# State times w_in formed once per batch, outputs accumulated tile by tile in a written order, weights converted on three engines

## The chip, the cores and the metric

The kernel runs on one core of one Trainium2 chip. The core has five engines that run side by side, each with its own strict queue: TensorE (PE; its weight loads are listed as PEld), VectorE (DVE), ScalarE (ACT), GpSimd (POOL) and SyncE (SP, which issues the transfers here). The metric is the device time of one execution in microseconds (us), lower is better. Before: 1142.45 us, the median of 3 runs (1141.72 to 1147.12).

## The reference

Two blocks. The first is a cross attention between 512 tokens and 32 state rows, for 8 batches and 8 heads of width 64, both ways round; the second is a feed-forward block with the gate h cos h over all 8 x (512 + 32) rows.

```python
# x (8, 8, 512, 64), state (8, 8, 32, 64): batch, head, row, width
scores = scale * np.matmul(x, state.transpose(0, 1, 3, 2))
a = softmax(scores)                       # over the 32 state rows
xread = np.matmul(a, state)
scores2 = scale * np.matmul(state, x.transpose(0, 1, 3, 2))
a2 = softmax(scores2)                     # over the 512 tokens
sread = np.matmul(a2, x)
attn = np.concatenate([xread, sread], axis=2)
# heads side by side: (8 * 544, 512)
x = attn.transpose(0, 2, 1, 3).reshape(B * S, H * D)
h = x @ w_in                              # w_in (512, 2048)
g = h * np.cos(h)
out = g @ w_out                           # w_out (2048, 512)
```

Everything is fp32 but w_in and w_out, which come as fp64 and are turned into fp32 on the chip.

## The kernel before, in words

**Attention** of a batch (`attention`, L120 to L233) transposes the states (L126) and the tokens (L134), forms the scores both ways (L150: state by token, L165: token by state), subtracts maxima, takes one Exp over both (L177), normalizes, and transposes the weights back (L197 into `a2T`, L205 into `aT`). L215 then reads tokens with the state's weights into `sT`, which collects what the states of all batches read. L228 multiplies the token's weights with the state: this gives `xx`, 512 features by 512 tokens, in four tiles of 128 features.

**Feed-forward** of a batch (`ffn`, L256). The hidden layer has 2048 features, in 16 tiles `f` of 128. For a tile, `gated` (L235) does four matmuls (L238), one for each 128 of the 512 contracted features, into a PSUM bank `hp`. The gate follows: DVE forms `q` (L242, L244) and `r` (L246, L248), ACT takes Abs and Sin (L250, L251), and DVE multiplies with `hp` into `g` (L253). All 16 `g` of a batch are kept (`gp` has 18 buffers). Then, for each 128 tokens, 16 matmuls (L265) add up one output tile in a PSUM bank; two banks are used in turn. ACT copies it out (L269) and SP stores it. After the eight batches the same is done for the 256 rows of `sT`, the state batch.

**Weights** (`load_w`, L89). A tile of 128 x 512 fp64 numbers is loaded as pairs of 32-bit words (`raw`, three buffers). Six DVE operations, one on ACT and one on POOL rebuild the number in fp32: `e` (L102, L104, L105, L107) carries sign and exponent, `fr` (L111, L112, L113) one plus the fraction, and POOL multiplies them (L115). There are 32 such tiles: 16 of `w_in` and 16 of `w_out`.

**Order.** The program writes attention of batch 0, the conversion of `w_in`, and then, for each batch, attention of the next batch before the feed-forward of this one; the conversion of one tile of `w_out` is written behind each hidden tile of batch 0. The framework's scheduler then sets the order on each engine. The PSUM banks are split 3 (`aps`, attention) + 3 (`hps`, hidden) + 2 (`ops`, outputs). SP's queue is written in the order: the first half of x of batch 0, states, the rest of it, weights, x of batch 1 between them; the loads of x (`load_x`, L78) for batch b + 2 are asked for at the start of batch b.

Of the kernel before, what the change touches and what calls it, by code (L numbers as in the profile page):

```python
# [9 lines left out]
F32 = mybir.dt.float32  # L10
# [16 lines left out]
def kernel(  # L27
# [18 lines left out]
    T = S + Ns            # tokens of a batch in the output  # L46
# [3 lines left out]
    wraw = ctx.enter_context(tc.tile_pool(name="wraw", bufs=3))  # L50
    xin = ctx.enter_context(tc.tile_pool(name="xin", bufs=3))
    asb = ctx.enter_context(tc.tile_pool(name="asb", bufs=1))
    small = ctx.enter_context(tc.tile_pool(name="small", bufs=2))
    xxp = ctx.enter_context(tc.tile_pool(name="xxp", bufs=2))
    gp = ctx.enter_context(tc.tile_pool(name="gp", bufs=NF + 2))
    msb = ctx.enter_context(tc.tile_pool(name="msb", bufs=2))
# [6 lines left out]
    halfpi = consts.tile([P, 1], F32)  # L63
    nc.vector.memset(halfpi, math.pi / 2.0)
# [3 lines left out]
    stB = consts.tile([P, B, NHB, 2 * D], F32)  # L68
    nc.vector.memset(stB, 0.0)
    st_src = state.rearrange("b (hb q) n d -> q n b hb d", q=4)  # L70
    for q in range(4):
        j = q % 2
        nc.sync.dma_start(out=stB[Ns * q:Ns * q + Ns, :, :, D * j:D * j + D],
                          in_=st_src[q])

# [11 lines left out]
    WC = 512  # L87

    def load_w(dst, src):  # L89
        """fp32 dst [P, WC] from src: fp32, or fp64 as its bits in 64-bit words."""  # L90
        if src.dtype == F32:
            nc.sync.dma_start(out=dst, in_=src)
            return
        raw = wraw.tile([P, WC, 2], I32, name="raw")
        nc.sync.dma_start(out=raw.rearrange("p f w -> p (f w)"),
                          in_=src.bitcast(I32))
        hi = raw[:, :, 1]
        lo = raw.bitcast(U32)[:, :, 0]
        # A power of two with the number's sign and exponent (zero below the
        # fp32 range, infinite above it), times 1 + its fraction.  # L100
        e = msb.tile([P, WC], I32, name="e", tag="q", bufs=3)
        nc.vector.tensor_scalar(e, hi, 20, 0x7FF, op0=ALU.logical_shift_right,  # L102
                                op1=ALU.bitwise_and)
        nc.vector.tensor_scalar(e, e, 896.0, 1151.0, op0=ALU.max, op1=ALU.min)  # L104
        nc.vector.tensor_scalar(e, e, 896.0, 2.0 ** 23, op0=ALU.subtract,  # L105
                                op1=ALU.mult)
        nc.vector.scalar_tensor_tensor(out=e, in0=hi, scalar=-2 ** 31, in1=e,  # L107
# [8 lines left out]

    # What attention writes to the state, of all batches: (j d) x pair x token.
    sT = consts.tile([P, NK, B, Ns], F32)

    def attention(b):  # L120
        x_b = x_t.pop(b)

# [208 lines left out]
```

## Time and profile before

| | |
|---|---|
| Time, median of 3 runs | 1142.45 us (1141.72 to 1147.12) |
| Profiled execution, first to last instruction | 1139.7 us |
| PE hidden matmuls, 128 x 512 (L238) | 1024 instructions, busy 448.8 us |
| PE output matmuls (L265) | 1088 instructions, busy 471.9 us |
| PE matmuls of L228 | 64 instructions, busy 23.4 us |
| DVE operations of conversion, L111 (the costliest) | 32, busy 26.2 us |
| POOL product, L115 | 32, busy 24.9 + 22.6 us |
| Bytes moved | 35.13 MB, mean 31 GB/s |

The profiled execution is one run of the program, and its span is the time from its first to its last instruction; the device time of a run also holds what lies around it. A busy time is the union of a group's instructions, a mean is the duration of one: PE's instructions overlap, so a mean of 592 ns does not say how far apart two of them start. An fp32 matmul stands as two instructions in the profile. In the list of groups, "xN" is the number of instructions, and what follows the second bar is the idle time of the engine before them with what ended it.

### The profile page before, as it was taken

How to read it: one execution, taken by the hardware profiler on the slowest of the kernel's cores; microseconds unless marked ns; L12 is line 12 of the kernel's file. 1: busy time of each engine (PE TensorE's matmuls, PEld its weight loads, DVE VectorE, ACT ScalarE, POOL GpSimd, SP SyncE). 2: the span in 40 equal slices, each digit the busy share in tenths (PEclk: the TensorE clock that was granted, in tenths of full speed). 3: DMA queues.
4: the chain of work that ended last, by engine and by line, in shares of the span. 5: the costliest groups of instructions: out<-in, count | busy, mean ns of one | idle time of the engine just before them, and what ended most of it. 6: DMA issues, size and time to landing. Idle time of an engine off the chain costs nothing.

```text
span 1139.7 us, 8231 instructions
## 1 busy us (share of the span) xinstructions
PE 1073.4 (94%) x3152; PEld 527.0 (46%) x3152; DVE 627.8 (55%) x1090; ACT 290.1 (25%) x440; POOL 48.2 (4%) x38
## 2 busy tenths in 40 slices
PE   3816999999999999999999999999999999999998
PEld 2504334554446444554455444544455444444483
DVE  6999998088107950488008830587028820791080
ACT  2313224043103320233013320243023310341041
POOL 1331222000000000000000000000000000000000
PEclk8967999999999999999999999999999999999999
DMA  9543221020001000010000000000000000000000
GB/s 203 156 138 93 92 93 38 18 37 1 9 19 39 8 8 20 10 37 1 18 19 1 0 10 18 10 1 1 18 19 1 0 10 18 10 0 17 20 1 19
DMA packets 45031, 35.13 MB, mean 31 GB/s; under 512 B 36544, under 2 KB 36544, under 8 KB 44992
## 3 DMA queue, kind: packets, MB, share of 16 engines
q1 hardware_dynamic: 44992, 34.61, 10.9%
q8 instruction: 25, 0.41, 0.2%
q14 instruction: 14, 0.11, 0.0%
HBM read 25.69 MB, written 8.91 MB: 30 GB/s over the span
## 4 chain that ended last, share of the span: by engine, by line
PE 84%; DVE 13%; issue 1%; DMA 1%; SPq 0%; ACT 0%; POOL 0%; ACTq 0%
PE o L265 39%; PE h L238 36%; PE at L215 2%; PE at L165 2%; DVE e L107 2%; PE at L228 2%; DVE e L104 1%; DVE fr L113 1%; DVE e L102 1%; PE at L150 1%; DVE e L105 1%; PE at L197 1%; DVE r L246 1%; PE at L134 1%; PE at L205 1%
## 5 line engine op out<-in xcount | busy, mean ns | idle before, releaser
L265 PE MATMUL o<-w_out,g 128*128 128x512 f32 x1088 | 471.9, 592 | 1.6 <-POOL w_out L115 1.6
L238 PE MATMUL h<-xx,w_in 128*128 128x512 f32 x1024 | 448.8, 595 | 4.8 <-DVE g L253 4.5
L265 PEld LDWEIGHTS o<-w_out,g 128*128 128x128 f32 x1088 | 206.4, 190 | 260.9 <-issue 255.9
L238 PEld LDWEIGHTS h<-xx,w_in 128*128 128x128 f32 x1024 | 191.8, 190 | 246.6 <-issue 214.3
L242 DVE TENSOR_SCALAR q<-h 128x512 f32<-128x512 f32 (+1 forms) x144 | 94.9, 659 | 131.3 <-PE h L238 128.8
L250 ACT ACTIVATE r<-r 128x512 f32<-128x512 f32 (+1 forms) x144 | 87.4, 607 | 297.2 <-DVE r L248 294.0
L128 DVE COPY stT<-at 128x256 f32<-128x256 f32 x8 | 3.4, 426 | 253.1 <-PE at L126 253.1
L269 ACT COPY ot<-o 128x512 f32<-128x512 f32 x34 | 19.9, 585 | 386.6 <-PE o L265 386.6
L253 DVE TENSOR_TENSOR g<-h,r 128x512 f32<-128x512 f32 (+1 forms) x144 | 94.9, 659 | 33.5 <-ACT r L251 31.1
L251 ACT ACTIVATE r<-r,halfpi 128x512 f32<-128x512 f32 (+1 forms) x144 | 100.6, 699 | 4.3
L248 DVE SCALAR_TENSOR_TENSOR r<-q,r 128x512 f32<-128x512 f32 (+1 forms) x144 | 95.0, 660 | 4.0
L246 DVE SCALAR_TENSOR_TENSOR r<-q,h 128x512 f32<-128x512 f32 (+1 forms) x144 | 93.5, 650 | 1.1
L244 DVE TENSOR_SCALAR q<-q 128x512 f32<-128x512 f32 (+1 forms) x144 | 58.7, 408 | 3.7
L197 PE MATMUL at<-ident,z 128*128 128x128 f32 x64 | 10.1, 310 | 42.6 <-DVE z L184 42.6
L165 PEld LDWEIGHTS at<-stT,xT 128*128 128x128 f32 x256 | 29.3, 192 | 8.5 <-PE at L150 5.7
L112 ACT ACTIVATE fr<-fr 128x512 f32<-128x512 int32 x32 | 19.9, 623 | 48.9 <-DVE fr L111 48.9
L156 DVE TENSOR_REDUCE mx<-at 128x1 f32<-128x512 f32 x16 | 11.0, 686 | 38.3 <-PE at L150 38.3
L232 ACT COPY xx<-at 128x512 f32<-128x512 f32 x32 | 17.6, 588 | 56.3 <-PE at L228 56.3
L165 PE MATMUL at<-stT,xT 128*128 128x64 f32 x256 | 30.6, 277 | 1.1 <-DVE z L157 1.1
L197 PEld LDWEIGHTS at<-ident,z 128*128 128x128 f32 x64 | 8.7, 161 | 46.7 <-issue 46.7
L215 PEld LDWEIGHTS at<-a2T,x_b 128*128 128x128 f32 x256 | 29.6, 193 | 0.5 <-DVE aT L207 0.3
L215 PE MATMUL at<-a2T,x_b 128*128 128x64 f32 x256 | 29.6, 274 | 0.0
(45 smaller groups left out, 482.0 us busy)
## 6 DMA issues: line engine op xcount, KB each, us to landing
x_b<-in_x_dram SPq DMA_DIRECT2D x32, 256.0 KB, 4.6
raw<-in_moe_w_in_dram SPq DMA_DIRECT2D x16, 512.0 KB, 4.1
raw<-in_moe_w_out_dram SPq DMA_DIRECT2D x16, 512.0 KB, 3.3
out_dram<-ot SPq DMA_DIRECT2D x32, 256.0 KB, 2.0
stB<-in_state_dram SPq DMA_DIRECT2D x4, 128.0 KB, 3.9
out_dram<-ot SPq DMA_DIRECT2D x8, 64.0 KB, 1.7
```

What stands on the lines that cost most here:

```text
L165: nc.tensor.matmul(out=s1[:, ci * H + 2 * k:ci * H + 2 * k + 2, :], lhsT=xT[:, k, CH * ch + ci, :], rhs=stT[:, k // 2, 64 * e:64 * e + 64] ...
L197: nc.tensor.transpose(out=tp[:, c, :], in_=z2[:, hb, P * c:P * c + P], identity=ident)
L215: nc.tensor.matmul(out=sr[:, k, :], lhsT=x_b[:, c, 2 * k:2 * k + 2, :], rhs=a2T[:, k // 2, c, 64 * e:64 * e + 64], start=(c == 0), stop=(c ...
L238: nc.tensor.matmul(out=hp, lhsT=w_in[:, k, P * f:P * f + P], rhs=xx[:, k, :], start=(k == 0), stop=(k == NK - 1))
L242: nc.vector.tensor_scalar(q, hp, 1.0 / (2.0 * math.pi), MAGIC, op0=ALU.mult, op1=ALU.add)
L244: nc.vector.tensor_scalar(q, q, MAGIC, None, op0=ALU.subtract)
L246: nc.vector.scalar_tensor_tensor(out=r, in0=q, scalar=-C1, in1=hp, op0=ALU.mult, op1=ALU.add)
L248: nc.vector.scalar_tensor_tensor(out=r, in0=q, scalar=-C2, in1=r, op0=ALU.mult, op1=ALU.add)
L250: nc.scalar.activation(r, r, func=ACTF.Abs)
L251: nc.scalar.activation(r, r, func=ACTF.Sin, bias=halfpi, scale=-1.0)
L253: nc.vector.tensor_tensor(g[:, 0:n], hp, r, op=ALU.mult)
L265: nc.tensor.matmul(out=op, lhsT=g[f][:, P * t:P * t + P], rhs=w_out[:, f, :], start=(f == 0), stop=(f == NF - 1))
```

## The change

- **Hidden layer.** Instead of forming `xx` = state x weights first and contracting it with `w_in` over 512 features, the state is multiplied with `w_in` once per batch (`products`, new L290): `sw`, 256 rows (head, state row) by 2048. The hidden matmuls (`hidden`, new L319) then contract the token's weights `aT` with `sw` over 256 rows, two matmuls a tile instead of four. L228 and its four copies on ACT are gone; eight product parts a batch and their eight copies on ACT (new L298) are new. The state batch still contracts `sT` with `w_in` over 512.
- **Outputs.** Four PSUM banks hold the four output tiles of a batch; as soon as a hidden tile has its `g`, four matmuls add its share to all four (`output`, new L352). `gp` has 4 buffers instead of 18. The banks are split 2 + 2 + 4.
- **Written order.** The scheduler is switched off, and the program's order is each engine's order. Attention is cut into 19 parts and the products into 8; for each hidden tile about 1.7 of these parts for the next batch are written between the steps: `gate3` of the tile before (its product with the Sin), `hidden`, `gate` (q), parts, `gate2` (r, Abs, Sin), `output` of the tile two back, parts.
- **Conversion.** ACT does three steps (a Relu for the exponent's lower bound, and the two halves of the fraction), POOL adds the halves and multiplies, DVE does four steps instead of six. The first half of a conversion is written with the second half of the one before. Four tiles of `w_in` are converted within attention of batch 0, and two tiles with each hidden tile of batch 0, `w_in` and `w_out` by turns. In batch 0 the subtraction of `q` is on ACT. `raw` has four buffers, `e`, `fr` and `fl` two each.
- **Loads.** The state loads stand first on SP, then x of batch 0, four weight tiles, x of batch 1; each further weight tile is fetched behind a conversion's second half. `x_b` has two buffers instead of three.

The core of the diff:

```diff
-    aps = ctx.enter_context(tc.tile_pool(name="aps", bufs=3, space=PSUM))
-    hps = ctx.enter_context(tc.tile_pool(name="hps", bufs=3, space=PSUM))
-    ops = ctx.enter_context(tc.tile_pool(name="ops", bufs=2, space=PSUM))
+    aps = ctx.enter_context(tc.tile_pool(name="aps", bufs=2, space=PSUM))
+    hps = ctx.enter_context(tc.tile_pool(name="hps", bufs=2, space=PSUM))
+    ops = ctx.enter_context(tc.tile_pool(name="ops", bufs=4, space=PSUM))
+    ctx.enter_context(tc.manual_schedule())
...
+            e = cvt.tile([P, WC], I32, name="e")
+            nc.vector.tensor_scalar(e, hi, 20, 0x7FF,
+                                    op0=ALU.logical_shift_right,
+                                    op1=ALU.bitwise_and)
+            nc.scalar.activation(e, e, func=ACTF.Relu, bias=ebias)
+            fr = cvt.tile([P, WC], F32, name="fr")
+            fi = fr.bitcast(I32)
+            nc.vector.tensor_scalar(fi, hi, 0xFFFFF, None, op0=ALU.bitwise_and)
+            nc.scalar.activation(fr, fi, func=ACTF.Copy, scale=2.0 ** -20,
+                                 bias=1.0)
+            fl = cvt.tile([P, WC], F32, name="fl")
+            nc.scalar.activation(fl, lo, func=ACTF.Copy, scale=2.0 ** -52)
+            half[i] = (hi, e, fr, fl)
+        if i - 1 in half:
+            hi, e, fr, fl = half.pop(i - 1)
+            nc.gpsimd.tensor_tensor(fr, fr, fl, op=ALU.add)
+            nc.vector.tensor_scalar(e, e, 255.0, 2.0 ** 23, op0=ALU.min,
+                                    op1=ALU.mult)
+            nc.vector.scalar_tensor_tensor(out=e, in0=hi, scalar=-2 ** 31,
+                                           in1=e, op0=ALU.bitwise_and,
+                                           op1=ALU.bitwise_or)
+            nc.gpsimd.tensor_tensor(loads[i - 1][0], fr, e.bitcast(F32),
+                                    op=ALU.mult)
+            fetch(i - 1 + 5)
...
+        def products(nt, hb):
+            ps = aps.tile([P, WC], F32, name="at")
+            for e in range(2):
                 nc.tensor.matmul(
+                    out=ps[64 * e:64 * e + 64, :],
+                    lhsT=stT[:, hb, 64 * e:64 * e + 64],
+                    rhs=w_in[:, 2 * hb + e, WC * nt:WC * nt + WC],
+                    start=True, stop=True, tile_position=(0, 64 * e))
+            nc.scalar.copy(sw[:, hb, WC * nt:WC * nt + WC], ps)
...
+    def output(t):
+        nt = t.n // P
+        if t.f == 0:
+            for i in range(nt):
+                acc[i] = ops.tile([P, Dm], F32, name="o")
+        for i in range(nt):
+            nc.tensor.matmul(out=acc[i], lhsT=t.g[:, P * i:P * i + P],
+                             rhs=w_out[:, t.f, :],
+                             start=(t.f == 0), stop=(t.f == NF - 1))
...
+        for t in tiles(b):
+            if line:
+                gate3(line[-1])
+            hidden(t)
+            gate(t)
+            line.append(t)
+            want = (len(work) * (t.f + 1) + NF - 1) // NF
+            mid = (n_done + want + 1) // 2
+            while n_done < mid:
+                work[n_done]()
+                n_done += 1
+            if b == 0:
+                convert_to(NK + 1 + 2 * (t.f + 1))
+                if t.f % 4 == 3:
+                    for part in first[:NHB]:
+                        part()
+                    first = first[NHB:]
+            gate2(t)
+            if len(line) > 2:
+                output(line.pop(0))
+            while n_done < want:
+                work[n_done]()
+                n_done += 1
```

Two places in the engines' orders. The first is TensorE's queue. Before, a whole batch from one L126 to the next (batch 2 and the attention of batch 3) stands as long runs; "at" are attention's PSUM tiles, "o" the outputs, and x50 is a run of 50 matmuls:

```order
L126 MATMUL at<-ident,stB 128x128 x2
L134 MATMUL at<-ident,x_b 128x128 x16
L150 MATMUL at<-xT,stT 64x512 x4
L165 MATMUL at<-stT,xT 128x64 x16
L238 MATMUL h<-xx,w_in 128x512 x13
L197 MATMUL at<-ident,z 128x128 x8
L238 MATMUL h<-xx,w_in 128x512
L205 MATMUL at<-ident,z 128x128 x8
L215 MATMUL at<-a2T,x_b 128x64 x16
L228 MATMUL at<-aT,stB 128x512 x4
L238 MATMUL h<-xx,w_in 128x512 x50
L265 MATMUL o<-w_out,g 128x512 x64
```

After, in the same queue, tiles 10 and 11 of a later batch with attention's last parts and the first products for the next (L278 is the old L215, L293 a product part, L322 the hidden and L358 the output matmuls):

```order
L322 MATMUL h<-aT,sw 128x512 x2
L278 MATMUL at<-a2T,x_b 128x64 x8
L358 MATMUL o<-w_out,g 128x512 x4
L278 MATMUL at<-a2T,x_b 128x64 x8
L322 MATMUL h<-aT,sw 128x512 x2
L293 MATMUL at<-w_in,stT 64x512 x2
L358 MATMUL o<-w_out,g 128x512 x4
L293 MATMUL at<-w_in,stT 64x512 x2
```

The runs of 64 hidden and 64 output matmuls have become groups of 2 and 4, with one part of the next batch's work behind each; L228 is gone, and L293 stands in its place.

The second place is VectorE's queue in batch 0, while weights are converted. Before, with the numbers of the buffers and the semaphores that each row waits for, one hidden tile and one conversion:

```order
L105 TENSOR_SCALAR e_779<-e_779 128x512 [waits DVE_49]
L111 TENSOR_SCALAR fr_784<-raw_777 128x512
L107 SCALAR_TENSOR_TENSOR e_779<-raw_777,e_779 128x512 [waits DVE_49]
L242 TENSOR_SCALAR q_794<-h_789 128x512 [waits PE_49,Pool_49]
L253 TENSOR_TENSOR g_775<-h_762,r_770 128x512 [waits Activation_49]
L113 SCALAR_TENSOR_TENSOR fr_784<-raw_777,fr_784 128x512 [waits Activation_49]
L244 TENSOR_SCALAR q_794<-q_794 128x512 [waits DVE_49]
L102 TENSOR_SCALAR e_806<-raw_804 128x512 [waits DMAHW0_49]
L246 SCALAR_TENSOR_TENSOR r_797<-q_794,h_789 128x512 [waits DVE_49]
L104 TENSOR_SCALAR e_806<-e_806 128x512 [waits DVE_49]
L248 SCALAR_TENSOR_TENSOR r_797<-q_794,r_797 128x512 [waits DVE_49]
```

After, one hidden tile (the eighth) with its two conversions, from its q on:

```order
L328 TENSOR_SCALAR q_725<-h_722 128x512 [waits PE_49]
L258 COPY a2T_333<-at_728 128x512 [waits PE_49]
L138 TENSOR_SCALAR e_734<-raw_658 128x512 [waits DMAHW3_49,Pool_49]
L144 TENSOR_SCALAR fr_737<-raw_658 128x512
L153 TENSOR_SCALAR e_697<-e_697 128x512
L155 SCALAR_TENSOR_TENSOR e_697<-raw_644,e_697 128x512 [waits DVE_49]
L138 TENSOR_SCALAR e_748<-raw_695 128x512 [waits DMAHW4_49,Pool_49]
L144 TENSOR_SCALAR fr_751<-raw_695 128x512
L153 TENSOR_SCALAR e_734<-e_734 128x512 [waits Activation_49]
L155 SCALAR_TENSOR_TENSOR e_734<-raw_658,e_734 128x512 [waits DVE_49]
L338 SCALAR_TENSOR_TENSOR r_770<-q_725,h_722 128x512
L340 SCALAR_TENSOR_TENSOR r_770<-q_725,r_770 128x512 [waits DVE_49]
```

Before, steps of the gate and of one conversion alternate, and a conversion's `e` waits only for its load; now the eight steps of two conversions stand between q and r, and each first step (L138) waits for POOL as well.

More of the change, by code (lines that the diff above doesn't have):

```diff
@@ new lines, in convert @@
+    def convert(i):
+        if not f64:
+            return
+        if i < len(loads):
+            raw = raws.pop(i)
+            hi = raw[:, :, 1]
+            lo = raw.bitcast(U32)[:, :, 0]
+            e = cvt.tile([P, WC], I32, name="e")
[22 more added lines that the diff above has]
+            fetch(i - 1 + 5)
@@ new lines, in reads @@
+        def reads(half):
+            if half == 0:
+                sr[0] = aps.tile([P, NK, 2 * Ns], F32, name="at")
+            for k in range(2 * half, 2 * half + 2):
+                e = k % 2
+                for c in range(NC):
+                    nc.tensor.matmul(
+                        out=sr[0][:, k, :], lhsT=x_b[:, c, 2 * k:2 * k + 2, :],
+                        rhs=a2T[:, k // 2, c, 64 * e:64 * e + 64],
+                        start=(c == 0), stop=(c == NC - 1))
+            if half == 0:
+                return
+            for j in range(2):
+                rows = slice(D * j, D * j + D)
+                nc.vector.tensor_copy(sT[rows, :, b, :],
+                                      sr[0][rows, :, Ns * j:Ns * j + Ns])
@@ L251, in gated @@
         nc.scalar.activation(r, r, func=ACTF.Sin, bias=halfpi, scale=-1.0)
[L252 to L270 removed]
+        t.r = r
@@ L304 @@
+    gate3(line[-1])
+    for t in line:
+        output(t)
 _INS = ['x', 'state', 'moe_w_in', 'moe_w_out']
```

301 lines of the change are left out of this document (168 added, 133 removed).

## The prediction

> **What bounds the kernel now.** I read the page's first two parts, then the chain that ended last, then busy time by stages that I cut by hand at the joints of the program, then TensorE's instructions in order of time.
>
> ```profile
> span 1139.7 us, 8231 instructions
> PE 1073.4 (94%) x3152; PEld 527.0 (46%) x3152; DVE 627.8 (55%) x1090; ACT 290.1 (25%) x440; POOL 48.2 (4%) x38
> PE   3816999999999999999999999999999999999998
> PEclk8967999999999999999999999999999999999999
> PE 84%; DVE 13%; issue 1%; DMA 1%; SPq 0%; ACT 0%; POOL 0%; ACTq 0%
> ...
> 0.00:36.70 36.70, 17.60 (x110) 14.96 (x110) 25.21 (x44) 7.55 (x10) 4.81 (x9) 0.86 0.82 184
> 36.70:195.00 158.30, 115.87 (x348) 54.28 (x346) 155.47 (x281) 49.56 (x79) 43.43 (x29) 0.89 0.33 100
> 195.00:340.51 145.51, 145.51 (x399) 68.41 (x399) 58.54 (x96) 31.37 (x45) 0.00 (x0) 1.00 0.07 20
> 466.34:592.17 125.83, 125.83 (x372) 60.90 (x371) 62.19 (x102) 32.21 (x47) 0.00 (x0) 1.00 0.07 17
> ```
>
> The last four rows are stretches with busy time of PE, PEld, DVE, ACT and POOL, the clock, and DMA. Two regimes show. Up to 195 us the weights are converted: DVE is busy 155.5 of 158.3 us, and nearly all of PE's 66 idle us lie before that point. From 195 us PE is busy in every microsecond at full clock, and DVE and ACT are half idle and a quarter busy. So behind 195 us time is worth what PE's instructions are worth; before it, what DVE's queue is worth.
>
> ```profile
> 466.34 0.38 PE L126 MATMUL at<-ident,stB 128*128 128x128 f32 x2
> 468.42 1.95 PE L150 MATMUL at<-xT,stT 128*64 128x512 f32 x8
> 491.36 2.92 PE L228 MATMUL at<-aT,stB 64*128 64x512 f32 x8
> 494.21 43.18 PE L238 MATMUL h<-xx,w_in 128*128 128x512 f32 x100
> 592.17 0.38 PE L126 MATMUL at<-ident,stB 128*128 128x128 f32 x2
> ...
> 969.64 55.10 PE L238 MATMUL h<-xx,w_in 128*128 128x512 f32 x128
> 1024.58 55.10 PE L265 MATMUL o<-w_out,g 128*128 128x512 f32 x128
> 1093.49 5.34 PE L238 MATMUL h<-sT,w_in 128*128 128x256 f32 x24
> 1098.67 1.02 PE L265 MATMUL o<-w_out,g 128*128 128x512 f32 x2
> ```
>
> An fp32 matmul is two instructions here: a batch has 16 x 4 hidden matmuls and 128 rows of L238. 128 of them take 1024.58 - 969.64 = 54.94 us, 0.429 us each; L265 costs the same. From one L126 to the next a batch takes 125.83 us. The state batch's 256-wide ones cost (1098.67 - 1093.49) / 24 = 0.216 us.
>
> **A batch on PE after.** The hidden layer contracts over 256 instead of 512: 64 instructions fewer, -64 x 0.429 = -27.5 us. L228 goes: -2.9 us. Added are 8 product parts, each two matmuls of 64 columns, that is four instructions. Their nearest row is L150, the same shape and the same column positions: 8 instructions in 1.95 us, so 0.98 us for four. That is about half of 4 x 0.429 = 1.72 us, so the two column halves run beside each other. Bounds 0.86 to 1.72 us a part; I take 1.0, since the shape is the same: +8 us. The parts of attention now stand singly between hidden and output matmuls. L150's 0.98 against 0.86 says that a change of shape costs about a tenth of a microsecond; ten such changes a batch beyond those of before are 1 us (0 to 4.5). Sum: 125.8 - 27.5 - 2.9 + 8 + 1 = 104.5 us, an estimate, 6.5 us a tile.
>
> This holds if the others keep up within a tile.
>
> ```profile
> L251 ACT ACTIVATE r<-r,halfpi 128x512 f32<-128x512 f32 x128 | 92.5, 723 | 3.8
> L248 DVE SCALAR_TENSOR_TENSOR r<-q,r 128x512 f32<-128x512 f32 x128 | 88.3, 690 | 3.8
> L253 DVE TENSOR_TENSOR g<-h,r 128x512 f32<-128x512 f32 x128 | 88.3, 689 | 32.5 <-ACT r L251 30.1
> L242 DVE TENSOR_SCALAR q<-h 128x512 f32<-128x512 f32 x128 | 88.1, 689 | 77.7 <-PE h L238 75.3
> L246 DVE SCALAR_TENSOR_TENSOR r<-q,h 128x512 f32<-128x512 f32 x128 | 86.8, 678 | 0.7
> L250 ACT ACTIVATE r<-r 128x512 f32<-128x512 f32 x128 | 80.8, 631 | 278.9 <-DVE r L248 275.8 <-DVE iz L181 3.1
> L244 DVE TENSOR_SCALAR q<-q 128x512 f32<-128x512 f32 x128 | 54.0, 422 | 3.2
> ```
>
> DVE was busy 62.19 us a batch, 3.9 us a tile. In the written order the last gate operation (g) waits for Abs and Sin of its own tile, 0.63 + 0.72 = 1.35 us, with the next tile's q queued behind it: at most 5.3 us of 6.5. The hidden result of tile t must be read by g before the hidden matmuls of t + 2 start, about 8.5 us after it was made (one tile and the next output); the chain q, q, r, r, Abs, Sin, g is 4.5 us, with a DVE part of attention 6. Outputs use g two tiles late. So I price waits of PE in batches 1 to 7 at nothing; the cover is those 2 to 3 us, and if it is gone each microsecond late costs one per tile. ACT gains 8 copies of about 0.6 us and loses 4: some 34 of 104 us. The four accumulators cost no instruction. At a batch's end the third copy on ACT waits for the first store, since there are two ot buffers; the next tile's Abs stands behind it. Copies are done before the next outputs need the banks, after a tile of 6.5 us. On SP the loads of x stand ahead of stores and are a batch early.
>
> Batches 1 to 6: 6 x 104.5 = 627 us. Batch 7 has no attention beside it: 64 x 0.429 + 128 x 0.429 = 82.4 us. The state batch does the same as before: 128 x 0.216 + 64 x 0.429 = 55.1 us.
>
> **Batch 0.** Tiles 0 to 13 each carry two conversions. Durations:
>
> ```profile
> L107 DVE SCALAR_TENSOR_TENSOR e<-raw,e x32: 621/679/1476, 14.5 to 189.2; 128x512 int32<-128x512 int32 x32
> L111 DVE TENSOR_SCALAR fr<-raw x32: 409/425/1503, 13.2 to 188.8; 128x512 int32<-128x512 int32 x32
> L104 DVE TENSOR_SCALAR e<-e x32: 411/418/1487, 13.5 to 187.1; 128x512 int32<-128x512 int32 x32
> L115 POOL TENSOR_TENSOR w_in<-fr,e x16: 1262/1380/2060, 16.4 to 84.5; 128x512 f32<-128x512 f32 x16
> ...
> L112 ACT ACTIVATE fr<-fr 128x512 f32<-128x512 int32 x32 | 19.9, 623 | 48.9 <-DVE fr L111 48.9
> ```
>
> The first four are minimum, median and maximum in ns. A DVE operation of 0.42 us stretches to 1.49, by about one POOL operation: the two exclude each other. After, POOL does two such operations a conversion, 1.38 us each, so this meets DVE more often. One more wait is new: e has two buffers, so the e of one conversion waits for POOL's product two conversions earlier, which by then has only just been allowed to start. Queued behind it on DVE is the rest of the tile, r and g included. DVE's tile then runs: g and q 0.69 + 0.69; first conversion 3 x 0.42 + 0.70 = 1.96; wait for POOL's product 1.38; second conversion 1.49 (its e meets POOL's addition, which follows at once) + 0.42 + 0.42 + 0.70; r and r 0.68 + 0.69, the second held 0.69 by POOL's next product (the kind of L107's 1.48); Abs and Sin 1.35 before the next g. That is 11.2 us. Attention adds 16 x (4 x 0.69 + 0.42) = 50.9 from 62.19, some 0.7 to 0.9 us a tile, about half under the wait for Sin: 11.5 us. Bounds: 9.8 if neither conversion nor r meets POOL, 15.8 if all six short operations take 1.49. I take 11.5. ACT's seven operations of 0.6 to 0.7 us, POOL's 4 x 1.38 = 5.5 us and PE's 6.5 us lie beside that, and 1 MB a tile is 91 GB/s where 184 was moved. The last two tiles convert nothing: 2 x 6.5. Batch 0: 14 x 11.5 + 13 = 174 us.
>
> **Start and end.**
>
> ```profile
> 0.74 1.07 SPq L82 DMA_DIRECT2D x_b<-in_x_dram  x2
> 3.06 1.93 SPq L73 DMA_DIRECT2D stB<-in_state_dram  x4
> ...
> 36.10 0.59 DVE L221 COPY sT<-at 64x128 f32<-64x128 f32 x2 [0.63 <-PE at L215]
> ...
> 1124.48 10.46 PE L265 MATMUL o<-w_out,g 128*128 128x512 f32 x24
> ...
> out_dram<-ot SPq DMA_DIRECT2D x32, 256.0 KB, 2.0
> ```
>
> Attention of batch 0 ends at 36.7 us with about as many conversions in it as after. After, all x loads stand behind the state loads, which wait for a memset: x goes from 0.74 to after 3.06, +2.3. Then a conversion's 1.96 on DVE, POOL's product 1.38, the product part 1.0 and a copy of 0.6: first hidden matmul at 44 us (40 to 48). At the end, 1139.7 - 1134.9 = 4.8 us follow the last matmul; two copies instead of one add 0.3.
>
> **Sum**: 44 + 174 + 627 + 82.4 + 55.1 + 5.2 = 988 us of span against 1139.7. The runs' median of 1142.45 lies 2.75 above the span; with the same around it: 991 us. Of the gain, 5 x 21.3 + 27.5 = 134 us lie behind 340 us and are PE's; the start gives only some 10 back, since the first 218 us are DVE's.
>
> [...] PE's clock in the stretches with gaps:
>
> ```profile
> 20.00:40.00 20.00, 11.24 (x66) 9.19 (x67) 19.16 (x36) 5.84 (x8) 3.74 (x3) 0.74 0.67 155
> 40.00:60.00 20.00, 16.97 (x74) 9.17 (x73) 19.97 (x34) 5.17 (x9) 8.09 (x6) 1.00 0.59 162
> 80.00:100.00 20.00, 6.31 (x36) 5.85 (x36) 19.93 (x35) 5.81 (x6) 2.64 (x2) 0.56 0.17 53
> ```
>
> At 56% busy the clock was 0.74, at 32% 0.56, at 85% whole. [...]
>
> **Rivals.**
> 1. *Conversions dearer* (15.8 us a tile): + 14 x 4.3 = 60, 1051 us. For: POOL's work doubles. Against: most rows of L111 and L104 stay at 0.42.
> 2. *Conversions cheaper* (9.8): - 14 x 1.7 = 24, 967 us.
> 3. *Products not side by side*: 64 x 0.72 = +46, 1037 us. Against: L150.
> 4. *The change doesn't give what it says, since the gate chain takes PE's place*: DVE's strict order makes PE wait in batches 1 to 7. At 0.5 us a tile, 112 x 0.5 = +56, 1047 us; no gain is left from 1.35 us a tile. For: parts of attention stand between q and r and before g. Against: 2 to 3 us of cover.
> 5. *Slower: the clock falls with the order*. Place: batches 1 to 8, 764 us of PE work at full clock. If short waits in each tile bring PE to the state of 20 to 40 us, 764 / 0.74 = 1032, +268, 1259 us. It decides against the change from a clock under 764 / (764 + 151) = 0.835, so somewhere between 56% and 85% busy. Against: I find PE over 95% busy there.
>
> **Chances.** Forecast 0.60, rivals in their order 0.12, 0.08, 0.04, 0.11, 0.05. Of rival 4, 0.02 lies near 1.35 us a tile and makes no difference. So faster by over 0.5% (about what a measurement tells from no change) 0.93, within 0.02, slower 0.05. The range leaves out rival 5 and the ends of 1 and 4: 955 to 1055.
>
> **What would show it.** In the profile after: L322 rows x512 at 0.43 us each and x256 of L293 at 0.25; batches 1 to 6 some 104 us apart with PE over 95% busy at clock 1.00 (rivals 4, 5); tiles of batch 0 11 to 12 us apart, DVE nearly full there with 1.4 to 1.5 us rows of L138 after waits for POOL (rivals 1, 2); the first L322 near 44 us. I am wrong if PE waits for g in most tiles of batches 1 to 7, or if batch 0 is far from 174 us.

## The result and the profile after

The changed kernel takes 1007.67 us (median of 4 runs, 1006.9 to 1007.94) against 1142.76 us before in the same session: ratio 0.8805, 95% interval 0.8783 to 0.8827. The forecast of 991 us was 17 us low, inside its range. From the page of the profile after, the lines that answer to those of before:

```profile
span 1005.8 us, 7676 instructions
PE 932.8 (93%) x2832; PEld 434.8 (43%) x2832; DVE 611.3 (61%) x1011; ACT 360.2 (36%) x554; POOL 88.3 (9%) x70
PE   4657768699999999999999999999999999999997
PEclk9576969799999999999999999999999999999999
PE 82%; DVE 10%; ACT 3%; POOL 2%; issue 1%; DMA 1%; SPq 0%; POOLq 0%; ACTq 0%
```

Each digit stands for 25.1 us. The first nine are the start and the batch with the conversions; behind them PE is busy at full clock without a break. The two regimes of before are still there, and the chain of work that ended last still runs through PE for 82% and DVE for 10%. To see where the sum was off I cut the span at the first hidden matmul of each batch (L322). The windows after (length, busy time of PE, PEld, DVE, ACT, POOL, clock, DMA share, GB/s), of the start, batch 0, batch 1, batch 7 and the state batch with the end:

```profile
0.00:50.20 50.20, 27.86 (x114) 18.52 (x114) 23.62 (x43) 14.77 (x22) 12.83 (x15) 0.76 0.54 134
50.20:222.60 172.40, 128.04 (x339) 52.25 (x339) 124.23 (x195) 93.27 (x150) 75.47 (x56) 0.83 0.30 86
222.60:328.00 105.40, 105.40 (x332) 48.08 (x331) 63.91 (x104) 36.21 (x53) 0.00 (x0) 1.00 0.08 20
854.70:937.90 83.20, 82.73 (x194) 36.43 (x193) 50.69 (x80) 22.94 (x35) 0.00 (x0) 1.00 0.04 13
937.90:1005.80 67.90, 62.12 (x209) 39.21 (x207) 32.53 (x81) 18.81 (x39) 0.00 (x0) 0.99 0.07 24
```

| stage | forecast, us | measured, us | off by |
|---|---|---|---|
| start, to the first L322 | 44 | 50.2 | +6.2 |
| batch 0 | 174 | 172.4 | -1.6 |
| batches 1 to 6 | 6 x 104.5 = 627 | 854.7 - 222.6 = 632.1 | +5.1 |
| batch 7 | 82.4 | 83.2 | +0.8 |
| state batch and end | 55.1 + 5.2 = 60.3 | 67.9 | +7.6 |

In the batch shown of 1 to 6, PE is busy in all of 105.40 us, DVE in 63.91. The step from 125.83 to 105.4 us a batch is the gain, and it lies where the prediction put it.

### The profile page after: what moved, and what is told of

Its sections match the earlier page's. It is cut to its first block, busy times and chain, and to the rows that moved or that the text cites. A ratio compares the mean times of both kernels' runs of the same rounds, so it can differ in the third digit from the quotient of the medians.

```text
span 1005.8 us, 7676 instructions
## 1 busy us (share of the span) xinstructions
PE 932.8 (93%) x2832; PEld 434.8 (43%) x2832; DVE 611.3 (61%) x1011; ACT 360.2 (36%) x554; POOL 88.3 (9%) x70
## 3 DMA queue, kind: packets, MB, share of 16 engines
q1 hardware_dynamic: 44992, 34.61, 12.3%
## 4 chain that ended last, share of the span: by engine, by line
PE 82%; DVE 10%; ACT 3%; POOL 2%; issue 1%; DMA 1%; SPq 0%; POOLq 0%; ACTq 0%
PE o L358 44%; PE h L322 23%; PE at L293 6%; PE at L278 3%; PE at L218 2%; DVE e L155 2%; DVE e L138 2%; DVE r L340 1%; POOL w_in L158 1%; PE at L204 1%; PE at L196 1%; DVE e L153 1%; DVE q L328 1%; DVE fr L144 1%; DVE r L338 1%
## 5 line engine op out<-in xcount | busy, mean ns | idle before, releaser
L358 PE MATMUL o<-w_out,g 128*128 128x512 f32 x1088 | 498.5, 600 | 0.5 <-ACT ot L364 0.5
L358 PEld LDWEIGHTS o<-w_out,g 128*128 128x128 f32 x1088 | 200.8, 191 | 250.4 <-issue 243.5
L322 PE MATMUL h<-aT,sw 128*128 128x512 f32 x512 | 251.5, 614 | 10.7 <-DVE g L348 10.7
L322 PEld LDWEIGHTS h<-aT,sw 128*128 128x128 f32 x512 | 93.2, 194 | 126.0 <-issue 88.7
L293 PE MATMUL at<-w_in,stT 128*64 128x512 f32 x256 | 82.4, 669 | 22.7 <-DVE a2T L258 6.6
L298 ACT COPY sw<-at 128x512 f32<-128x512 f32 x64 | 37.0, 583 | 128.1 <-PE at L293 128.1
L293 PEld LDWEIGHTS at<-w_in,stT 128*64 128x64 f32 x256 | 14.8, 143 | 80.0 <-issue 57.2
L152 POOL TENSOR_TENSOR fr<-fr,fl 128x512 f32<-128x512 f32 x32 | 47.4, 1480 | 18.6 <-ACT fl L148 18.6
L141 ACT ACTIVATE e<-e,ebias 128x512 int32<-128x512 int32 x32 | 23.1, 721 | 52.7 <-DVE e L138 52.7
L138 DVE TENSOR_SCALAR e<-raw 128x512 int32<-128x512 int32 x32 | 26.1, 815 | 24.1 <-POOL w_in L158 17.4
L278 PEld LDWEIGHTS at<-a2T,x_b 128*128 128x128 f32 x256 | 34.3, 210 | 7.5 <-issue 7.2
L278 PE MATMUL at<-a2T,x_b 128*128 128x64 f32 x256 | 33.6, 290 | 0.0
L196 PE MATMUL at<-ident,x_b 128*128 128x128 f32 x128 | 22.3, 303 | 11.8 <-ACT xT L199 9.5
```

Source lines behind the costliest of these rows:

```text
L278: nc.tensor.matmul(out=sr[0][:, k, :], lhsT=x_b[:, c, 2 * k:2 * k + 2, :], rhs=a2T[:, k // 2, c, 64 * e:64 * e + 64], start=(c == 0), stop ...
L293: nc.tensor.matmul(out=ps[64 * e:64 * e + 64, :], lhsT=stT[:, hb, 64 * e:64 * e + 64], rhs=w_in[:, 2 * hb + e, WC * nt:WC * nt + WC], star ...
L322: nc.tensor.matmul(out=t.hp, lhsT=t.lhs(i), rhs=t.rhs(i), start=(i == 0), stop=(i == t.kn - 1))
L358: nc.tensor.matmul(out=acc[i], lhsT=t.g[:, P * i:P * i + P], rhs=w_out[:, t.f, :], start=(t.f == 0), stop=(t.f == NF - 1))
```

## Experiments

All of them compute the whole output. Times are medians, and ratios are to the kernel before, run beside them on the same chip, in three sets (before: 1143.28, 1142.52 and 1146.36 us). Within one set the kernel before spread from 1141.0 to 1147.9 us, so differences of 3 or 4 us between runs of different sets are weak evidence.

### What the contraction alone is worth

The contraction over 512 is put back (`xx` from state and weights, w_in as the other operand); written order, four accumulators, conversion and loads stay.

```diff
-        def products(nt, hb):
-            ps = aps.tile([P, WC], F32, name="at")
...
-            nc.scalar.copy(sw[:, hb, WC * nt:WC * nt + WC], ps)
+        def expand(k):
+            rows = slice(64 * (k % 2), 64 * (k % 2) + 64)
+            y = aps.tile([P, S], F32, name="at")
+            nc.tensor.matmul(
+                out=y, lhsT=stB[rows, b, k // 2, :],
+                rhs=aT[rows, k // 2].rearrange("p c t -> p (c t)"),
+                start=True, stop=True, tile_position=(64 * (k % 2), 0))
+            nc.scalar.copy(xx[:, k, :], y)
...
-                t.n, t.kn, t.store = S, NHB, store_x(b)
+                t.n, t.kn, t.store = S, NK, store_x(b)
```

> The contraction over 512 is put back: state times token weights (four matmuls a batch, as L228 before) and four hidden matmuls a tile; the written order, the four accumulating banks and the conversion stay. Theory (batches 1 to 7 are TensorE's instructions): batches 1 to 6 gain 64 x 0.429 = 27.5 and 2.9 us and lose the products, 8 x 1.2 = 9.6: +20.8 each; batch 7 +27.5; batch 0 unchanged within 10: 1008 + 125 + 27 = 1160 us, above the kernel before. Rival (the gain is from the written order and the banks): under 1060 us.

Measured: 1173.33 us (1173.08 to 1173.59), ratio 1.0255 (1.0218 to 1.0293): slower than before. Start 50.4, batch 0 174.6, a later batch 128.2, batch 7 109.9, state batch 68.0. One later batch in a window of that kernel:

```profile
353.20:481.30 128.10, 128.10 (x371) 60.12 (x370) 63.42 (x103) 32.70 (x47) 0.00 (x0) 1.00 0.07 17
```

PE is the bound in both forms, with nothing idle, and 128.2 - 105.3 = 22.9 us a batch are the shorter contraction's (20.8 were expected). In this kernel it is worth 1173.3 - 1007.7 = 166 us; everything else in the change, taken together, costs about 30 us against the kernel before.

A batch of this kernel is also 2.4 us longer than the 125.8 of before. TensorE's order of time in it shows most of why:

```profile
455.71 3.60 PE L320 MATMUL h<-xx,w_in 128*128 128x512 f32 x8
459.24 1.12 PE L293 MATMUL at<-aT,stB 64*128 64x512 f32 x2
460.29 3.70 PE L356 MATMUL o<-w_out,g 128*128 128x512 f32 x8
463.92 1.12 PE L293 MATMUL at<-aT,stB 64*128 64x512 f32 x2
```

A single `expand` takes 460.29 - 459.24 = 1.05 us. Eight full-width instructions need 8 x 0.429 = 3.43 us; with an `expand` behind them they take 459.24 - 455.71 = 3.53, with one on both sides 463.92 - 460.29 = 3.63. Each `expand` beside such a group so adds 0.10 us to it, ahead or behind, and one `expand` costs 1.05 + 0.20 = 1.25 us, four 5.0; before, the four stood together in 494.21 - 491.36 = 2.85 us. That is 2.0 to 2.2 of the 2.4 us; the rest was not looked for.

### What sets batch 0: the order on DVE

In batch 0 the second conversion of each tile, and the products that need it, are written behind `gate2` instead of ahead of it. DVE's wait for Sin and POOL's product can then pass under other work.

```diff
             if b == 0:
-                convert_to(NK + 1 + 2 * (t.f + 1))
+                convert_to(NK + 2 + 2 * t.f)
+            gate2(t)
+            if b == 0:
+                convert_to(NK + 1 + 2 * (t.f + 1))
                 if t.f % 4 == 3:
...
-            gate2(t)
```

> In batch 0 the second conversion of a tile, and the products of every fourth tile, are written behind the r steps instead of before them. Theory (a tile of batch 0 is DVE's queue with its two waits, 1.44 us for POOL's product and 1.45 us for Sin): both waits fall under other DVE work. A tile is then 0.69 + 0.69 + 1.96 + 0.68 + 1.33 + 1.47 + 1.53 = 8.4 us and 0.8 us of attention, 9.2 us in place of 11.65; 14 tiles give 34 us, so about 974 us. Rival (TensorE's wait for the products at tiles 3, 7 and 11, or the transfer of the weights, sets batch 0): under 10 us, 1000 us or more. Batches 1 to 8 stay as they are in both.

Measured: 990.99 us (990.65 to 991.48), ratio 0.8662 (0.8641 to 0.8683). Batch 0 takes 156.5 us instead of 172.4, all else is the same: the place was right, the size about half of that expected. First, VectorE's order of time in the changed kernel, one tile of batch 0 from q to q:

```profile
64.59 0.68 DVE L328 TENSOR_SCALAR q<-h 128x512 f32<-128x512 f32 x1
...
66.31 0.69 DVE L155 SCALAR_TENSOR_TENSOR e<-raw,e 128x512 int32<-128x512 int32 x1
68.46 1.47 DVE L138 TENSOR_SCALAR e<-raw 128x512 int32<-128x512 int32 x1 [1.45 <-POOL w_in L158]
...
71.96 1.33 DVE L340 SCALAR_TENSOR_TENSOR r<-q,r 128x512 f32<-128x512 f32 x1
74.74 0.69 DVE L348 TENSOR_TENSOR g<-h,r 128x512 f32<-128x512 f32 x1 [1.45 <-ACT r L343]
75.35 0.68 DVE L328 TENSOR_SCALAR q<-h 128x512 f32<-128x512 f32 x1
```

This is the tile that the prediction walked through: a wait of 1.45 us for POOL's product, an `e` stretched to 1.47, an r stretched to 1.33, a wait of 1.45 for Sin. With the order changed:

```profile
64.52 1.33 DVE L340 SCALAR_TENSOR_TENSOR r<-q,r 128x512 f32<-128x512 f32 x1
65.77 1.50 DVE L138 TENSOR_SCALAR e<-raw 128x512 int32<-128x512 int32 x1
...
68.58 0.68 DVE L348 TENSOR_TENSOR g<-h,r 128x512 f32<-128x512 f32 x1
```

g follows without a wait. From q to q, eleven of the 14 converting tiles fall from 11.2 us on average to 9.3, the 9.2 of the expectation. Tiles 3, 7 and 11 do not follow: they took 14.5, 13.1 and 12.3 us and now take 14.0 to 14.2, and that is where the other half went. Behind each of them the next hidden matmuls need products whose w_in tile has only just been converted. In order of time, the end of tile 3 in the changed kernel:

```profile
91.36 1.97 PE L293 MATMUL at<-w_in,stT 128*64 128x512 f32 x2 [1.10 <-POOL w_in L158]
93.26 5.60 PE L358 MATMUL o<-w_out,g 128*128 128x512 f32 x8
98.69 1.88 PE L322 MATMUL h<-aT,sw 128*128 128x512 f32 x4
...
100.61 0.69 DVE L328 TENSOR_SCALAR q<-h 128x512 f32<-128x512 f32 x1 [2.30 <-PE h L322]
```

The last product waits 1.10 us for POOL, the eight output instructions behind it take 5.4 us at a clock of 0.65 (3.43 at full clock), and DVE then waits 2.30 us for the hidden ones. So the late product and PE's low clock both have a share here, and they were not taken apart. This second cost of batch 0 is no step of the prediction.

### Both costs of batch 0 taken away by hand

On top of that, products stand ahead of the tile's first conversion in tiles 3, 7 and 11, and the order of the weight tiles is changed so that they are converted by then.

```diff
-    for a, b in zip(in_tiles[NK:], out_tiles):
-        loads += [a, b]
-    loads += out_tiles[len(in_tiles) - NK:]
+    for n in range(NT - 1):
+        i4 = in_tiles[NK * (n + 1):NK * (n + 2)]
+        o4 = out_tiles[NK * n:NK * (n + 1)]
+        loads += [i4[0], i4[1], o4[0], i4[2], i4[3], o4[1], o4[2], o4[3]]
+    loads += out_tiles[NK * (NT - 1):]
```

> As the kernel with the second conversion behind the r steps, and the products of tiles 3, 7 and 11 stand first in their tile; the weight tiles of w_in are loaded and converted two by two ahead of those of w_out, so that the last one a product needs is ready a tile earlier. Theory (in that kernel tiles 3, 7 and 11 took 14 us instead of 9 because the next hidden tile waits for products, these for the conversion just behind them in POOL's queue, and the copies for three ACT steps of a conversion): these tiles fall to 9.5 to 10 us, batch 0 takes 14 x 9.5 + 13 = 146 us instead of 172, about 981 us. Rival (something else in these tiles, the transfers or the clock of TensorE): 988 us or more, as the split alone. Both conversions' waits stay as there.

Measured: 982.28 us (981.24 to 982.87), ratio 0.859 (0.8569 to 0.861). Batch 0: 147.9 us; tiles 3, 7 and 11 now take 10.6, 10.3 and 12.7, where 9.5 to 10 were expected. Each of the two costs shrinks when its order is changed. The place of the products and the order of the weights changed together, so their shares are not known, nor why tile 11 stays long.

### Is it the wait for POOL, or the exclusion?

`e` and `fr` get a third buffer, and q and r go from three to two to make room, so no `e` waits for an older product.

```diff
-            e = cvt.tile([P, WC], I32, name="e")
+            e = cvt.tile([P, WC], I32, name="e", bufs=3)
...
-            fr = cvt.tile([P, WC], F32, name="fr")
+            fr = cvt.tile([P, WC], F32, name="fr", bufs=3)
...
-        q = msb.tile([P, S], F32, name="q")[:, 0:t.n]
+        q = msb.tile([P, S], F32, name="q", bufs=2)[:, 0:t.n]
...
-        r = msb.tile([P, S], F32, name="r")[:, 0:t.n]
+        r = msb.tile([P, S], F32, name="r", bufs=2)[:, 0:t.n]
```

> e and fr have three buffers instead of two (room comes from q and r, two instead of three), so that the first step of a conversion no longer waits for POOL's product of the conversion before. Theory A (the semaphore wait of 1.44 us costs by itself): 14 x 1.4 = 20 us less, 988 us. Theory B (the exclusion of DVE's short operations while POOL runs would hold the same step as long anyway): L138 starts earlier but takes until POOL's product ends, 1.4 to 1.5 us, and the time stays within 5 us of 1008; between them if L138 then gets in before POOL's addition, 14 x 1.05 = 15 us less.

Measured: 1004.61 us (1004.11 to 1005.36), ratio 0.8781 (0.876 to 0.8802); batch 0 169.9 us. VectorE's order of time in that kernel:

```profile
76.21 0.42 DVE L138 TENSOR_SCALAR e<-raw 128x512 int32<-128x512 int32 x1
76.55 1.51 DVE L144 TENSOR_SCALAR fr<-raw 128x512 int32<-128x512 int32 x1
77.97 1.50 DVE L153 TENSOR_SCALAR e<-e 128x512 int32<-128x512 int32 x1
```

The 1.45 us wait and the stretched `e` are gone, and two later operations of 0.42 us now take 1.5 each. Over batch 0, DVE's waits for POOL fall from 18.8 us to none and its busy time rises from 124.2 to 137.7 us. POOL's product and its addition hold DVE for about the same time whichever of DVE's operations comes (2.2 us of stretches against 1.45 + 1.05); the wait for the buffer only named one of them. That is theory B by the time, though it was not L138 that was held. POOL's two operations stand at 76.44 (1.33 us) and 77.72 (1.46 us), and each stretched DVE operation begins just after one of them and ends 0.3 us after it. In the changed kernel the `e` at 68.46 (1.47 us) begins 0.08 us after POOL's addition at 68.38 (1.27 us) and ends 0.28 us after it. Not every DVE operation is held so: a reduction (L210) at 83.96, within POOL's addition at 83.45 (1.71 us), took its 0.68 us. What tells the two apart is not shown.

### The three-engine conversion in the written order

The conversion of before (six operations on DVE, one each on ACT and POOL) is put into the changed kernel's places.

```diff
-            nc.scalar.activation(e, e, func=ACTF.Relu, bias=ebias)
+            nc.vector.tensor_scalar(e, e, 896.0, 1151.0, op0=ALU.max,
+                                    op1=ALU.min)
...
-            fl = cvt.tile([P, WC], F32, name="fl")
-            nc.scalar.activation(fl, lo, func=ACTF.Copy, scale=2.0 ** -52)
...
-            nc.vector.tensor_scalar(e, e, 255.0, 2.0 ** 23, op0=ALU.min,
+            nc.vector.tensor_scalar(e, e, 896.0, 2.0 ** 23, op0=ALU.subtract,
...
+            nc.vector.scalar_tensor_tensor(out=fr, in0=fl, scalar=2.0 ** -52,
+                                           in1=fr, op0=ALU.mult, op1=ALU.add)
```

> Conversion as before the change, six DVE operations, one on ACT and one on POOL, in the written order. Theory (waits and POOL's exclusion eat what the two operations taken off DVE gave): a conversion is 3.1 us of DVE work instead of 1.96, +2.2 us a tile, but the second one no longer meets POOL's addition, -1.05: about +1 us a tile, 14 to 16 us, 1023 us. Rival (DVE's work sets batch 0): +2.2 us a tile, +31 us, 1039 us or more. If conversion by three engines was worth nothing: 1008 or less.

Measured: 1031.1 us (1027.4 to 1032.57), ratio 0.9002 (0.897 to 0.9035). Start +3.6, batch 0 +21.1 us (193.5). The time lies between the theory's 1023 and the rival's 1039. In this order the three-engine conversion saves 23 us.

### The written order against the scheduler

The one line that switches the scheduler off is taken out of the changed kernel.

```diff
-    ctx.enter_context(tc.manual_schedule())
```

> The same program with the framework's scheduler instead of the written order. Theory (behind batch 0 TensorE's instructions set the time, whatever their order): batches 1 to 7 stay within 2 us of 105 and the whole within 20 us of 1008. Rival (the written order carries a good part of the gain): 1040 us or more.

Measured: 976.24 us (975.37 to 977.11), ratio 0.8539 (0.8513 to 0.8565): 31 us faster than the change, which neither theory had. Batches 1 to 6 take 105.3 us as in the written order; batch 0 takes 144.4:

```profile
48.40:192.80 144.40, 121.64 (x340) 50.25 (x339) 121.55 (x187) 89.34 (x146) 73.52 (x52) 0.93 0.33 98
```

DVE does about the same work (121.55 against 124.23 us busy), but is idle for 22.9 instead of 48.2 us. A tile of batch 0 in VectorE's order of time, with the scheduler:

```profile
63.12 0.68 DVE L327 TENSOR_SCALAR q<-h 128x512 f32<-128x512 f32 x1
63.72 0.68 DVE L347 TENSOR_TENSOR g<-h,r 128x512 f32<-128x512 f32 x1
64.66 1.48 DVE L137 TENSOR_SCALAR e<-raw 128x512 int32<-128x512 int32 x1 [0.26 <-POOL w_in L157]
...
66.73 0.67 DVE L337 SCALAR_TENSOR_TENSOR r<-q,h 128x512 f32<-128x512 f32 x1
67.33 0.68 DVE L154 SCALAR_TENSOR_TENSOR e<-raw,e 128x512 int32<-128x512 int32 x1
67.93 1.75 DVE L339 SCALAR_TENSOR_TENSOR r<-q,r 128x512 f32<-128x512 f32 x1
```

g of the tile before stands behind q of the next, so Sin is done when g comes, and a conversion step lies between the two r. The stretches are still there; the waits are halved: over batch 0, DVE's waits for POOL fall from 18.8 to 9.5 us, for Sin from 16.1 to 6.7, and for the hidden matmuls from 8.7 to 2.8.

> The old conversion (six DVE operations) with the scheduler. Theory (where waits are hidden, DVE's work and its meetings with POOL set batch 0): +2.2 us of work a tile, less up to 1.05 for the missing addition: 14 x 1.2 to 2.2 = 16 to 31 us above the scheduler's 976, 992 to 1007 us. Rival (batch 0 is then set by TensorE or by loads): within 5 us of 976.

This is the scheduler with the conversion of before (the two diffs above together). Measured: 978.93 us (978.75 to 979.11), ratio 0.8556 (0.8519 to 0.8594). The time is within the rival's 5 us, but by two changes that nearly cancel: without the three-engine conversion the first hidden matmul comes 7 us earlier (41.6), and batch 0 is longer by 9 (153.3). With the scheduler that conversion is worth at most 2 to 3 us, not 23; the two runs are of different sets, and the intervals of their ratios overlap.

### How much cover PE has in batches 1 to 7

One, then three more DVE additions (on a tile of zeros of their own) in each hidden tile of batches 1 to 7, ahead of `gate2`; q goes from three buffers to two.

```diff
+            if 0 < b < B:
+                for _ in range(1):
+                    nc.vector.tensor_tensor(padt, padt, padt, op=ALU.add)
             gate2(t)
```

> One more DVE operation of 0.6 us per tile in batches 1 to 7, between q and r (it adds a tile of zeros to itself). Theory (DVE has 63.3 / 16 = 4.0 us of work and at most 1.45 us of wait for Sin in a tile that TensorE needs 6.6 us for, 5.2 in batch 7): 6.0 us a tile fits; 0 to 5 us more, 1008 to 1013 us. Rival (the gate chain already sets the pace of batches 1 to 7): 0.6 x 112 = 67 us more.

> Three more DVE operations, 1.9 us per tile, at the same place. Theory: 5.4 + 1.9 = 7.3 us exceeds TensorE's 6.6 in batches 1 to 6, +0.7 x 96 = 66 us, and 4.6 + 1.9 = 6.5 its 5.2 in batch 7, +21 us: 1095 us, 1060 at least, since part of the wait for Sin lies under attention's steps. Rival (TensorE has far more cover, since two hidden banks and two tiles of delay decouple it): 1008 to 1020 us.

Measured with one: 1015.51 us (1014.93 to 1016.1), ratio 0.8883 (0.8856 to 0.8909), 7.8 us more than the change, a little above the 0 to 5 expected; with three: 1092.97 us (1091.88 to 1094.06), ratio 0.956 (0.953 to 0.959), 85 us more, as expected, 0.76 a tile for about 2 us of work. What PE waited for between 222 and 950 us in the kernel with one (time in total, number of waits, longest):

```profile
PE at L266 <- DVE z L248: 5.4, 6, 0.9
```

And in the kernel with three, where batch 7 starts at 919.7 us and most of it lies behind 950:

```profile
PE at L266 <- DVE z L248: 24.2, 6, 4.0
PE o L360 <- ACT ot L366: 16.9, 14, 3.0
PE h L324 <- DVE g L350: 8.3, 12, 1.1
```

The first place to give way is one step of attention a batch: the transposes of the weights (L266) wait for DVE's normalization (L248). The hidden matmuls wait for g most of all in batch 7: its tiles first follow each other at 5.15 us but for one wait for a copy, and from the eighth on at 6.58, each with a wait of 1.16 us for g. There the gate chain sets the pace once the lead of the first tiles is used up. Up to the state batch at 1020.6 us the waits for g are 19.9 us in all, and the three kinds sum to 61 of the 85 us; the clock was 0.97 in the batch that I cut out, and the rest was not traced.

### The start

Loads of x of batch 0 are put ahead of the states' again: first in the written order, then in the fastest version (scheduler and the changed weight order together).

```diff
+    load_x(0)
     st_src = state.rearrange("b (hb q) n d -> q n b hb d", q=4)
     for q in range(4):
...
-    load_x(0)
```

> The changed kernel with x of batch 0 loaded ahead of the states, which wait for a memset (before the change its first half was). Theory (the order of these loads costs the start 2.3 us): the tokens' transposes end 2 to 3 us earlier and the first hidden matmul with them, 1005 us. Rival (the start is late because TensorE runs it at half clock and ACT's third and fourth copy stand behind a conversion, whatever lands first): within 1 us of 1008.

> The order of weights of e8, with the scheduler instead of the written order. Theory (the scheduler hides the waits of a tile, and the three tiles that wait for products are what it can't hide, since the weights come in the same order): those tiles fall by some 2 us each, 970 us. Rival (the scheduler's batch 0 is at DVE's own work and POOL's exclusion, about 9.3 us a tile): within 3 us of 976.

> e10 with x of batch 0 ahead of the states: 2 to 3 us less than e10 if the start's loads count, the same if not.

Measured: 1007.27 us (1006.06 to 1007.75), ratio 0.8802 (0.8777 to 0.8828): no change. x comes earlier, the states later, and PE's first instruction, which needs the states, starts at 11.27 instead of 8.40 us; the first hidden matmul comes at 49.08 instead of 50.21. Since both loads moved, this does not show what x's later load costs by itself. Scheduler and weight order together: 973.29 us (972.53 to 975.17), ratio 0.8509 (0.8483 to 0.8535), the fastest measured here, but within the 3 us of the scheduler alone that the rival allowed; x first in it: 977.77 us (974.97 to 977.93), ratio 0.8538 (0.8506 to 0.857), no gain. In the profiles PE starts 2.2 us later there (10.82 against 8.63), its first hidden matmul 2.7 us later (51.23 against 48.52), and the span is 2.7 us longer.

## Why the prediction was right, and where its sum was off

**A batch on PE: right.** PE bounds batches 1 to 6 with nothing idle, as forecast, and putting the 512 back returns 22.9 us a batch. The mis-sized term is that of the changes of shape. TensorE's order of time after:

```profile
320.51 1.08 PE L293 MATMUL at<-w_in,stT 128*64 128x512 f32 x4
321.52 1.98 PE L322 MATMUL h<-aT,sw 128*128 128x512 f32 x4
323.44 1.08 PE L293 MATMUL at<-w_in,stT 128*64 128x512 f32 x4
324.45 3.70 PE L358 MATMUL o<-w_out,g 128*128 128x512 f32 x8
327.98 1.88 PE L322 MATMUL h<-aT,sw 128*128 128x512 f32 x4
329.70 0.38 PE L189 MATMUL at<-ident,stB 128*128 128x128 f32 x2
```

The product takes 1.01 us, the 1.0 of the forecast; the third rival (1.72) is out. But the hidden matmuls between two products take 323.44 - 321.52 = 1.92 us, against 329.70 - 327.98 = 1.72 between full-width groups, and the outputs with a product on one side only take 327.98 - 324.45 = 3.53, against 3.43. Each side of a product costs the tenth of a microsecond of the forecast; but eight products have sixteen sides, and the sum had ten changes of shape in all. A product so costs 1.2 us, eight 9.6, where the forecast had 8 + 1. That is 0.6 of the 0.8 us a batch; the rest was not added up.

**Batch 0: right on average, with one step missing.** Forecast 11.5 us a converting tile, measured 163.1 / 14 = 11.65 between the first steps of q. The single waits and stretches are those of the working. But tiles 3, 7 and 11, which wait for products, take 13.3 us on average and the other eleven 11.2. The working had no step for the three; its allowance for attention happened to cover it, so that the average came out is in part luck. The last two tiles took 4.8 us each, not 6.5. The first two rivals (15.8 and 9.8 a tile) did not come. One sign was named wrongly: DVE is not "nearly full" there but busy in 124.23 of 172.40 us, and the working's own two waits (1.38 + 1.35 of 11.2 us) already left a quarter of a tile idle.

**State batch and end: a term in the wrong stage.** "The state batch does the same as before: 55.1 us" left out the lag. Outputs run two tiles behind hidden tiles, so at the first L322 of the state batch two tiles of output of batch 7 are still to do: 2 x 8 x 0.429 = 6.9 us. The sum gave those two to batch 0, whose first two tiles have no output to do; DVE sets the pace there, so that saves nothing. 55.1 + 6.9 = 62.0, and PE was busy 62.12 us there. The remaining 5.8 us follow the last matmul (forecast 5.2): both output tiles of the state batch end there, and their eight stores follow, where before only the last tile's four were left.

**Start: 6.2 us short, and outside the 40 to 48 given for it.** The forecast added x's later load, 2.3 us, to the old start. TensorE's order of time after:

```profile
15.86 3.46 PE L204 MATMUL at<-xT,stT 128*64 128x512 f32 x8
...
36.21 1.94 PE L264 MATMUL at<-ident,z 128*128 128x128 f32 x8 [2.67 <-DVE z L246]
38.08 7.09 PE L278 MATMUL at<-a2T,x_b 128*128 128x64 f32 x32
```

The same three groups before:

```profile
13.02 1.95 PE L150 MATMUL at<-xT,stT 128*64 128x512 f32 x8
...
30.49 1.91 PE L205 MATMUL at<-ident,z 128*128 128x128 f32 x8
32.20 3.87 PE L215 MATMUL at<-a2T,x_b 128*128 128x64 f32 x32
```

The scores (L204) start 2.8 us later than before, near the 2.3. The transposes (L264) start 5.7 us later: another 2.9 us come in with a wait for DVE's normalization (L246). Before, that step stood right behind the other normalization on DVE, at 28.93 us after 28.14; after, four conversion steps and two copies lie between the two, at 30.96 and 34.69. The reads (L278) then take 7.09 us instead of 3.87, 3.2 more. So attention ends about 9 us later where the sum had 2.3, and about 0.5 us is saved behind it. The longer L204 (3.46 for 1.95) is not among these: the first transposes behind the scores were 2.8 us late like the scores themselves. The windows give the clock: 0.96 between 32 and 40 us before; after:

```profile
32.00:40.00 8.00, 5.33 (x25) 4.62 (x24) 6.66 (x13) 3.40 (x6) 3.57 (x3) 0.50 0.19 68
40.00:50.20 10.20, 9.85 (x33) 6.01 (x32) 2.72 (x7) 2.46 (x5) 4.79 (x4) 0.54 0.31 94
```

The sum held the start's matmuls at their old durations, although the prediction itself showed clocks of 0.74 and 0.56 in stretches of before in which PE was busy for 56% and 32%, and it held DVE's order there as it was, although the written order changes it. What keeps the clock low there was not tried.

**The rivals in batches 1 to 7.** The gate chain did not take PE's place: the whole list of PE's waits there holds one, of 0.5 us. With 0.6 us more of DVE work a tile still no hidden matmul waits for g, so the cover claimed for the gate held; but attention's normalization, a place the working did not price, gave way already. Nor did the clock fall with the order: it is 1.00 while PE visits four accumulators tile by tile, and groups of different banks follow one another without idle time (105.40 of 105.40 us busy). That short waits in each tile would bring PE to the clock of 0.74 was the author's estimate from the stretch of 20 to 40 us before; such waits did not come here, and in the kernel with three more additions a tile, with PE busy for 109.03 of the 116.60 us of a batch, the clock was 0.97.

**What the prediction did not ask** is what each part is worth. Each was measured by taking it out of the changed kernel: the contraction gives 166 us, the rest of the change together costs 30, and the written order costs 31 against the scheduler, 28 of them in batch 0. These need not add up; the contraction alone, put into the kernel before, was not run.

## What to carry to other kernels

Where one engine is busy without a break, a change is worth its instructions on that engine, counted with the loss at each change of shape (about 0.1 us on each side here); where an engine's queue has waits in it, ask first whether another order hides them. Measure the parts of a change that comes as a bundle apart: here one part made all the gain and another gave a fifth of it back. When work is delayed by a fixed lag, book the lag in the stage that ends with it.

## What the runs showed of the hardware beyond the expected

- A full-width group beside matmuls that use half of the array's rows or columns takes about 0.1 us longer for each such neighbour, ahead of it or behind it (four instructions 1.72 with none and 1.92 with two; eight 3.43, 3.53 and 3.63). The half-width work itself is longer by 0.15 to 0.19 us than its instructions' share (1.01 and 1.05 against 0.86), so a single excursion costs some 0.35 us. Bundled it is cheaper: the four matmuls of the old L228 took 2.85 us together and cost 1.25 each standing alone.
- More buffers hardly shortened DVE's time beside POOL (3 us of the whole): short DVE operations met POOL's in either case, and stretched from 0.42 to 1.5 us.
- PE's clock was 0.50 from 38 to 48 us though PE was busy in 10.00 of these 10.00 us (7.09 us for 32 matmuls that took 3.87 before), 0.67 from 48 to 50 us, and 1.00 again only from 50 to 56 us; before, PE was busy without a break from 28.8 us, and the clock was 0.50 up to 32 us, 0.85 from 32 to 34 and 1.00 from 34 to 40 us. What tells the two apart is not shown.
